# First FFN product of the last two token groups by Strassen's scheme, ELUs issued between the additions

## The chip, the cores and the metric

One core of a Trainium2 chip. The metric is the device time of one execution in microseconds (us); lower is better. PE is TensorE, DVE VectorE, ACT ScalarE, POOL GpSimd. PSUM is the memory, in banks, in which matmuls are summed; SBUF is the core's other memory. The granted clock is the share of its full clock that the profile shows TensorE to have had. A slack is the time by which something could come later before PE would wait.

## The reference

An attention with a threshold, then an FFN with ELU over its 4608 output rows of 512. The change concerns the FFN alone:

```python
n_tokens, d_model, d_ff = (4608, 512, 2048)
def _moe_ref(x, w_in, w_out):
    h = x @ w_in                                                     # first product
    g = np.where(h > 0.0, h, alpha * (np.exp(np.minimum(h, 0.0)) - 1.0))   # ELU, alpha = 1
    return (g @ w_out).astype(np.float32)                            # second product
```

## The kernel before

Tokens come in nine groups of 512: eight sequences, and a ninth group of the 64 last tokens of each. A group's FFN is interleaved with the next group's attention, except for the last two groups, which are left over at the end. A group is two chunks `c` of 256 tokens. `ffn1` is the plain first product, with the f tiles `u` and `u + 8` side by side; `ffn2` is the second product, by Strassen's scheme already.

```python
def ffn1(c, u):                                  # cut
    def part(k):                                 # k = 0, 1: f tile u, u + 8
        for j in range(KJ):                      # KJ = 4 tiles of d_model
            nc.tensor.matmul(loc["ph"][:, k], w_in_sb[:, j, ft * P : (ft + 1) * P],
                             xts[g][:, j, hf * CT : (hf + 1) * CT], start=(j == 0), stop=(j == KJ - 1))
    def exp():
        nc.scalar.activation(loc["g"], loc["h"], AF.Exp)                     # h is in PSUM
    def minus():
        nc.gpsimd.tensor_scalar(loc["g"], loc["g"], 1.0, -1.0, ALU.mult, ALU.add)
    def elu():
        nc.vector.scalar_tensor_tensor(loc["g"], loc["g"], 0.0, loc["h"], ALU.min, ALU.max)
        if u % 2 and c >= PLAIN:
            sums(c, u - 1)                       # four GpSimd sums for Strassen's second product

# the end of the program, after the last attention step
xts[B] = xpool.tile([P, KJ, MAIN], FP32, name="xt")
nc.sync.dma_start(xts[B], xtail.rearrange("j p n -> p j n"))
push_ffn(B)
while pending or units:
    finish_units(ffn_halves(1), slice(0, None))
    run_extra(99)
```

## Time and profile before

| | before |
|---|---|
| time, median of the first 3 runs | 1455.3 us (1453.4 to 1457.4) |
| profiled run | span 1449.4 us, granted clock 0.995 |
| last attention output copied (the last xt copy on ScalarE) | 1235.9 us |
| from there to the end of the span | 213.5 us |
| first and second product of a chunk in that stretch | 27.63 us and 24.17 us, PE alone |

### The profile page before, as it was taken

Reading aid. Unit: us, or ns where it says so; the run is one execution under the profiler, and the core shown is the slowest. Engines: PE = TensorE matmul, PEld = TensorE weight load, DVE = VectorE, ACT = ScalarE, POOL = GpSimd, SP = SyncE. Lnnn points to the kernel's source line nnn. Section 1 sums busy time; section 2 is a strip of 40 time slices with the busy share of each in tenths; the row PEclk is TensorE's granted clock in tenths of the full one; section 3 lists DMA queues with packets and bytes.
Section 4 is the critical chain, followed back from the end, with each engine's and each line's share of the span. In section 5 each row is a group of like instructions: output and inputs, shape, how many; then the busy total and the mean of one; then the engine's idle time right before and its main releaser. Section 6 shows DMA issues by size and latency. Waiting matters only on the chain.

```text
span 1449.4 us, 20329 instructions
## 1 busy us (share of the span) xinstructions
PE 1391.5 (96%) x6822; PEld 1037.2 (72%) x6822; DVE 878.9 (61%) x1910; ACT 439.7 (30%) x780; POOL 667.7 (46%) x1194
## 2 busy tenths in 40 slices
PE   7988778999999999999999999999999999999998
PEld 4555534647777777777777777777777778888887
DVE  6887665567676766677676767676767674111111
ACT  5665554323222322223222323232323231100100
POOL 4665554546444454535363626363535443313422
PEclk9999899999999999999999999999999999999999
DMA  4344442177677676667676767666767765100000
GB/s 95 78 93 117 111 123 84 51 193 188 184 185 195 174 202 183 190 181 185 183 197 171 189 190 191 182 189 180 195 182 192 192 172 148 45 15 8 8 15 15
DMA packets 298903, 205.44 MB, mean 142 GB/s; under 512 B 206384, under 2 KB 270384, under 8 KB 298800
## 3 DMA queue, kind: packets, MB, share of 16 engines
q1 hardware_dynamic: 298800, 204.15, 52.9%
q8 instruction: 54, 0.88, 0.2%
q14 instruction: 49, 0.40, 0.1%
HBM read 119.87 MB, written 84.21 MB: 141 GB/s over the span
## 4 chain that ended last, share of the span: by engine, by line
PE 82%; DVE 8%; POOL 4%; ACT 3%; issue 2%; DMA 1%; SPq 0%; POOLq 0%; DVEq 0%; ACTq 0%
PE ph L393 33%; PE po L494 24%; PE sc L220 12%; PE pv L347 8%; DVE w L247 2%; PE pv L343 2%; PE po L459 2%; ACT e L235 2%; POOL wtop L141 2%; DVE mx L230 2%; PE rt L259 1%; POOL w L256 1%; DVE wtop L136 1%; POOL nb L231 1%; DVE w_out_sb L145 1%
## 5 line engine op out<-in xcount | busy, mean ns | idle before, releaser
L393 PE MATMUL ph<-xt,w_in_sb 128*128 128x256 f32 x2304 | 521.5, 383 | 3.5 <-DVE w_in_sb L145 3.5
L393 PEld LDWEIGHTS ph<-xt,w_in_sb 128*128 128x128 f32 x2304 | 433.3, 190 | 83.9 <-issue 21.0
L235 ACT ACTIVATE e<-sc,nb,keep 128x576 f32<-128x576 f32 x288 | 227.6, 829 | 439.2 <-POOL nb L231 438.0
L230 DVE TENSOR_REDUCE mx<-sc 128x2 f32<-128x1152 f32 (+1 forms) x176 | 199.9, 1136 | 229.1 <-PE sc L220 229.0
L256 POOL TENSOR_SCALAR w<-w,rs 128x576 f32<-128x576 f32 x288 | 219.1, 771 | 223.5 <-DVE rs L250 217.3
L247 DVE SCALAR_TENSOR_TENSOR w<-sc,th,e 128x576 f32<-128x576 f32 x288 | 226.8, 815 | 78.3 <-ACT e L235 53.8
L220 PE MATMUL sc<-kT,qT 64*128 64x288 f32 x1024 | 180.3, 437 | 18.9 <-DVE w L247 9.1
L404 POOL TENSOR_SCALAR g<-g 128x512 f32<-128x512 f32 x144 | 89.7, 623 | 200.5 <-ACT g L401 199.3
L307 DVE STREAM_TRANSPOSE x<-w 128x512 f32<-128x512 f32 (+1 forms) x350 | 181.2, 567 | 0.9 <-POOL w L256 0.9
L231 POOL TENSOR_SCALAR nb<-mx,nkeep 128x2 f32<-128x2 f32 (+1 forms) x176 | 51.7, 294 | 265.1 <-DVE mx L230 257.6
L401 ACT ACTIVATE g<-ph 128x512 f32<-128x512 f32 x144 | 86.0, 597 | 266.2 <-PE ph L393 266.2
L408 DVE SCALAR_TENSOR_TENSOR g<-g,ph 128x512 f32<-128x512 f32 x144 | 97.0, 674 | 112.7 <-POOL g L404 112.6
L220 PEld LDWEIGHTS sc<-kT,qT 64*128 64x128 f32 x1024 | 99.3, 189 | 86.0 <-issue 53.1
L494 PE MATMUL po<-t,s 128*128 128x256 f32 x512 | 122.8, 386 | 4.5 <-DVE u L514 4.5
L494 PE MATMUL po<-w_out_sb,s 128*128 128x256 f32 x512 | 120.1, 384 | 0.0
L494 PE MATMUL po<-w_out_sb,g 128*128 128x256 f32 x512 | 117.7, 379 | 0.0
L494 PEld LDWEIGHTS po<-t,s 128*128 128x128 f32 x512 | 94.5, 190 | 28.9 <-DVE u L514 8.9
L494 PEld LDWEIGHTS po<-w_out_sb,s 128*128 128x128 f32 x512 | 95.4, 190 | 19.7 <-issue 4.7
L494 PEld LDWEIGHTS po<-w_out_sb,g 128*128 128x128 f32 x512 | 97.3, 190 | 13.9
L424 POOL TENSOR_TENSOR s<-g 128x256 f32<-128x256 f32 x128 | 93.2, 728 | 12.9 <-DVE g L408 12.9
L347 PE MATMUL pv<-wTb,vm 128*64 128x320 f32 x512 | 76.7, 439 | 0.0
L350 ACT COPY xt<-pv 128x256 f32<-128x256 f32 x64 | 23.8, 372 | 159.3 <-PE pv L347 159.2
(64 smaller groups left out, 1129.0 us busy)
## 6 DMA issues: line engine op xcount, KB each, us to landing
there<-x SPq DMA_DIRECT2D x500, 144.0 KB, 3.5
wTb<-there SPq DMA_DIRECT2D x75, 576.0 KB, 4.4
wTa<-there SPq DMA_DIRECT2D x50, 576.0 KB, 3.7
qm<-in_q_dram SPq DMA_DIRECT2D x128, 72.0 KB, 2.6
km<-in_k_dram SPq DMA_DIRECT2D x128, 72.0 KB, 3.6
vm<-in_v_dram SPq DMA_DIRECT2D x64, 128.0 KB, 2.5
wst<-in_moe_w_in_dram SPq DMA_DIRECT2D x16, 512.0 KB, 4.2
wst<-in_moe_w_out_dram SPq DMA_DIRECT2D x16, 512.0 KB, 3.8
```

Of the source, the lines that this page charges most:

```text
L220: nc.tensor.matmul(scs[h][:, a, :HALF], qs[r], kT[r, k0 : k0 + HALF], start=True, stop=True)
L230: nc.vector.tensor_reduce(st["mx"][:, cs], src[:, :, :, :HALF], axis=AX.XY, op=ALU.max)
L235: nc.scalar.activation(e, st[h][:, :, :HALF], AF.Exp, bias=st["nb"][:, h : h + 1], scale=keep)
L247: nc.vector.scalar_tensor_tensor(wv, sc[:, :, :HALF], st["th"][:, h : h + 1], e, ALU.is_ge, ALU.mult, accum_out=sm[:, h : h + 1])
L256: nc.gpsimd.tensor_scalar(wv, wv, st["rs"][:, h : h + 1], 1.0, ALU.mult, ALU.mult)
L307: nc.vector.transpose(x[:, :, c0 : c0 + nc_], src.rearrange("p (c g n) -> p g c n", c=nc_, n=T))
L347: nc.tensor.matmul(pv[h * D : (h + 1) * D, g0 * T : g1 * T], vm[:, h, c], wT[:, g0:g1, h * (NC + 1) + c], start=False, stop=(c == NC - 1), ...
L393: nc.tensor.matmul(loc["ph"][:, k], w_in_sb[:, j, ft * P : (ft + 1) * P], xts[g][:, j, hf * CT : (hf + 1) * CT], start=(j == 0), stop=(j = ...
L404: nc.gpsimd.tensor_scalar(loc["g"], loc["g"], 1.0, -1.0, ALU.mult, ALU.add)
L408: nc.vector.scalar_tensor_tensor(loc["g"], loc["g"], 0.0, loc["h"], ALU.min, ALU.max)
L424: nc.gpsimd.tensor_tensor(out, x, y, op)
L494: nc.tensor.matmul(cur[c, place], lhs, rhs, start=(begins and u == 0), stop=(u == NU - 1), skip_group_check=True)
```

## The change

Intent: for each pair of f tiles and all 512 tokens of a group, seven products of half size in place of eight. The sums of weights are made by VectorE late in the attention loop (six pairs) and inside the first group (two pairs), those of the inputs at the head of the first group and, for the second, under the first one's second product. Three accumulators X, Y, Z, each a whole PSUM bank, six banks in all. Each pair's exp and ELU are put off into the next pair. The core of the diff:

```diff
+        def first_product(g, u):
+            X, Y, Z = (psum["f"].tile([P, 512], FP32, name="po", tag="f")[:, :CT] for i in range(3))
+            h = hs[u % 2]                               # in SBUF
             ... # product(): two matmuls of 256 columns; kept(): copy or addition out of PSUM into SBUF
+            rest("exp0")                                # of the pair before, as all rest()
+            product(a11, b11, X, True)                  # 1
+            p1 = kept("s1", X)
+            rest("exp1")
+            product(a22, t4, Z, True)                   # 2
+            w1 = kept("w1", Z, p1)
+            rest("elu0")
+            product(a12, b21, X, False)                 # 3
+            nc.scalar.copy(h[:, 0, 0], X)
+            product(s2, t2, Y, True)                    # 4
+            u2 = kept("u2", Y, p1)
+            product(s1, t1, Z, True)                    # 5
+            t5 = kept("t5", Z, p1)
+            rest("elu1")
+            product(s3, t3, Y, False)                   # 6
+            nc.vector.tensor_tensor(h[:, 0, 1], Y, w1, ALU.add)
+            nc.vector.tensor_tensor(h[:, 1, 1], Y, t5, ALU.add)
+            product(s4, b22, Z, False)                  # 7
+            nc.vector.tensor_tensor(h[:, 1, 0], Z, u2, ALU.add)
             ...
-        push_ffn(B)
         while pending or units:
             finish_units(ffn_halves(1), slice(0, None))
             run_extra(99)
+        banks.close()
+        psum["f"] = ctx.enter_context(tc.tile_pool(name="ps_f3", bufs=6, space=PSUM))
+        input_sums(B - 1)                               # four 512-wide sums on VectorE
+        for g in (B - 1, B):
+            for u in range(NU):
+                if g < B and u in (2, 4):
+                    first_sums(u // 2 + 5)              # four weight sums of one pair
+                first_product(g, u)
+            flush()
             ... # then the second product; the odd chunk's sums are now on VectorE (3 of 4) and GpSimd
```

More of the change, by code (lines that the diff above doesn't have):

```diff
@@ L397, in exp @@
             if u == 0:
-                gs[c] = gpool.tile([P, NU, 2, 2, P], FP32, name="g")
-            loc["g"] = gs[c][:, u].rearrange("p j i t -> p (j i t)")
+                gs[c] = [gpool.tile([P, NU, 2, 2, P], FP32, name="g")]
+            loc["g"] = hidden(c, u, 1).rearrange("p u j i t -> p (u j i t)")
             loc["h"] = loc["ph"].rearrange("p k t -> p (k t)")
@@ L412, in ffn1, with hidden, sums @@
         return [lambda: part(0), lambda: part(1)], (exp, minus, elu)
-    def sums(c, u):
-        g = gs[c]
+    def hidden(c, u, n):
+        for g in gs[c]:
+            if u < g.shape[1]:
+                return g[:, u : u + n]
+            u -= g.shape[1]
+    def sums(c, u, engines=(nc.gpsimd,) * 4):
+        g = hidden(c, u, 2)
         def one(k):
@@ L419, in one @@
                 ss[c] = late["x"].tile([P, 4, NU, P], FP32, name="s", bufs=1)
-            (a11, a21), (a12, a22) = ([g[:, u : u + 2, j, i] for i in range(2)] for j in range(2))
+            (a11, a21), (a12, a22) = ([g[:, :, j, i] for i in range(2)] for j in range(2))
             s1, s2, s3, s4 = (ss[c][:, i, u : u + 2] for i in range(4))
@@ L423, in one @@
                              (s3, a11, a21, ALU.subtract), (s4, a12, s2, ALU.subtract))[k]
-            nc.gpsimd.tensor_tensor(out, x, y, op)
+            engines[k].tensor_tensor(out, x, y, op)
         extra.extend((0.8, c, lambda k=k: one(k)) for k in range(4))
@@ L458, in run @@
             for ft in range(4 * part + 2 * k, 4 * part + 2 * k + 2):
-                nc.tensor.matmul(cur[c, i][:, :DM], gs[c][:, ft % NU, ft // NU, i], w_out_sb[:, ft],
+                nc.tensor.matmul(cur[c, i][:, :DM], hidden(c, ft % NU, 1)[:, 0, ft // NU, i], w_out_sb[:, ft],
                                  start=(ft == 0), stop=(ft == NFT - 1))
@@ L488, in part @@
             for u in range(k * NU // 2, (k + 1) * NU // 2):
-                lhs = gs[c][:, u, left[1], left[2]] if left[0] == "g" else ss[c][:, left[1], u]
+                lhs = hidden(c, u, 1)[:, 0, left[1], left[2]] if left[0] == "g" else ss[c][:, left[1], u]
                 if right[0] == "w":
@@ L548, in behind @@
             values(pr, 0 if i == 1 else 1)
-        if i == NB - 1 and (pr + 1) % NPAIR == 0:
+        if i == NB - 1 and (pr + 1) % NPAIR == 0 and pr + 1 < NP:
             push_ffn(pr // NPAIR)
@@ L648 @@
     for name, bufs in (("s", 1), ("f", 3), ("t", 1)):
-        psum[name] = ctx.enter_context(tc.tile_pool(name=f"ps_{name}2", bufs=bufs, space=PSUM))
+        psum[name] = banks.enter_context(tc.tile_pool(name=f"ps_{name}2", bufs=bufs, space=PSUM))
     early.close()
@@ L654, with pieces_of, first_rooms, first_sums @@
         weight_sums(u, False)
+    def pieces_of(pool, name, shape, n, times=1, bufs=None):
+        for _ in range(times):
+            t = pool.tile(shape, FP32, name=name, bufs=bufs)
+            if len(shape) > 2:
+                axes = " ".join("abc"[: len(shape) - 1])
+                t = t.rearrange(f"p {axes} -> p ({axes})")
+            for x in range(0, t.shape[1] - n + 1, n):
+                yield t[:, x : x + n]
+    QN = 2 * P
+    rooms = []
+    def first_rooms():
+        rooms[:] = [*pieces_of(raw, "qm", [P, S // T, T], QN), *pieces_of(raw, "km", [P, S // T, T], QN),
+                    *pieces_of(qkp, "qT", [P, S], QN, 2), *pieces_of(qkp, "kT", [P, TAIL + S], QN, 2),
+                    *pieces_of(att, "e", [P, 2, HALF], QN, 2), *pieces_of(wpool[0], "w", [P, 2 * S], QN)]
+    sums_in = {}
+    def first_sums(u):
+        f0, f1 = (slice(f * P, (f + 1) * P) for f in (u, NU + u))
+        a11, a12, a21 = w_in_sb[:, :2, f0], w_in_sb[:, 2:, f0], w_in_sb[:, :2, f1]
+        s1, s2, s4 = sums_in[u] = [rooms.pop(0).rearrange("p (k f) -> p k f", k=2) for _ in range(3)]
+        nc.vector.tensor_tensor(s1, a21, w_in_sb[:, 2:, f1], ALU.add)
+        nc.vector.tensor_tensor(s2, s1, a11, ALU.subtract)
+        nc.vector.tensor_tensor(a21, a11, a21, ALU.subtract)
+        nc.vector.tensor_tensor(s4, a12, s2, ALU.subtract)
     QUOTA = ((2, 2), (2, 2), (2, 0), (2, 1), (2, 0))
@@ L672 @@
             run_extra(3.0)
+            if n > len(steps):
+                if n == len(steps) + 1:
+                    first_rooms()
+                for u in range(3 * (n - len(steps) - 1), 3 * (n - len(steps))):
+                    first_sums(u)
             if SWITCH < n <= len(steps):
@@ L693 @@
         finish_units(after, slice(0, None))
-        xts[B] = xpool.tile([P, KJ, MAIN], FP32, name="xt")
-        nc.sync.dma_start(xts[B], xtail.rearrange("j p n -> p j n"))
-        push_ffn(B)
         while pending or units:
@@ L699 @@
             run_extra(99)
+        banks.close()
+        psum["f"] = ctx.enter_context(tc.tile_pool(name="ps_f3", bufs=6, space=PSUM))
+        wide, narrow = wtp.tile([P, 3 * NT, NCH, T], FP32, name="wTb"), wtp.tile([P, 2 * NT, NCH, T], FP32, name="wTa")
+        wide, narrow = (t.rearrange("p g c n -> p (g c n)") for t in (wide, narrow))
+        g2 = [t.rearrange("p (u j i t) -> p u j i t", j=2, i=2, t=P) for t in (wide[:, : 12 * QN], narrow[:, : 4 * QN])]
+        rooms += [wide[:, 12 * QN : 13 * QN], narrow[:, 8 * QN : 9 * QN], *pieces_of(raw, "vm", [P, 2, NC, D], QN, bufs=2)]
@@ new lines, with input_sums @@
+        t2, t4 = (narrow[:, x * QN : (x + 2) * QN].rearrange("p (k t) -> p k t", k=2) for x in (4, 6))
+        (t3,) = pieces_of(raw, "vm", [P, 2, NC, D], 2 * QN, bufs=2)
+        t3 = t3.rearrange("p (k t) -> p k t", k=2)
+        hs = [h.rearrange("p (c j t) -> p c j t", c=2, j=2) for h in pieces_of(late["x"], "x", [P, NT, NCH, T], 4 * QN, 2, 2)]
+        def input_sums(g):
+            (b11, b12), (b21, b22) = ([xts[g][:, k : k + 2, t : t + CT] for t in (0, CT)] for k in (0, 2))
+            nc.vector.tensor_tensor(t3, b22, b12, ALU.subtract)
+            nc.vector.tensor_tensor(t2, t3, b11, ALU.add)
+            nc.vector.tensor_tensor(t4, b21, t2, ALU.subtract)
+            nc.vector.tensor_tensor(b12, b12, b11, ALU.subtract)
@@ new lines, in first_product, with product, kept, rest @@
+        def first_product(g, u):
+            f0, f1 = (slice(f * P, (f + 1) * P) for f in (u, NU + u))
+            (b11, t1), (b21, b22) = ([xts[g][:, k : k + 2, t : t + CT] for t in (0, CT)] for k in (0, 2))
+            s1, s2, s4 = sums_in[u]
+            a11, a12, s3, a22 = w_in_sb[:, :2, f0], w_in_sb[:, 2:, f0], w_in_sb[:, :2, f1], w_in_sb[:, 2:, f1]
+            X, Y, Z = (psum["f"].tile([P, 512], FP32, name="po", tag="f")[:, :CT] for i in range(3))
+            h = hs[u % 2]
+            def product(left, right, place, begins):
+                for k in range(2):
+                    nc.tensor.matmul(place, left[:, k], right[:, k], start=(begins and k == 0), stop=(k == 1),
+                                     skip_group_check=True)
+            def kept(name, x, y=None):
+                t = epool.tile([P, HM], FP32, name=name)
+                if y is None:
+                    nc.scalar.copy(t, x)
+                else:
+                    nc.vector.tensor_tensor(t, x, y, ALU.add)
+                return t
+            def rest(name):
+                if name in open_rest:
+                    open_rest.pop(name)()
+            rest("exp0")
[17 more added lines that the diff above has]
+            nc.vector.tensor_tensor(h[:, 1, 0], Z, u2, ALU.add)
+            def exp(c):
+                gt = hidden(2 * g + c, u, 1).rearrange("p u j i t -> p (u j i t)")
+                hc = h[:, c].rearrange("p j t -> p (j t)")
+                nc.scalar.activation(gt, hc, AF.Exp)
+                nc.gpsimd.tensor_scalar(gt, gt, 1.0, -1.0, ALU.mult, ALU.add)
+                open_rest[f"elu{c}"] = lambda: elu(c, gt, hc)
+            def elu(c, gt, hc):
+                nc.vector.scalar_tensor_tensor(gt, gt, 0.0, hc, ALU.min, ALU.max)
+                if c == 0 and u % 2:
+                    sums(2 * g, u - 1)
+                    run_extra(99)
+            open_rest["exp0"] = lambda: exp(0)
+            open_rest["exp1"] = lambda: exp(1)
@@ new lines, with flush @@
+        open_rest = {}
+        def flush():
+            for name in ("exp0", "exp1", "elu0", "elu1"):
+                open_rest.pop(name)()
+        input_sums(B - 1)
+        xts[B] = xpool.tile([P, KJ, MAIN], FP32, name="xt")
+        nc.sync.dma_start(xts[B], xtail.rearrange("j p n -> p j n"))
+        for g in (B - 1, B):
+            gs[2 * g] = [gpool.tile([P, NU, 2, 2, P], FP32, name="g")]
+            gs[2 * g + 1] = g2
+            for u in range(NU):
[3 more added lines that the diff above has]
+            flush()
+            for c in (2 * g, 2 * g + 1):
+                units.extend((ffn2, (c, m)) for m in range(7))
+                if c % 2:
+                    for u in range(0, NU, 2):
+                        sums(c, u, (nc.vector, nc.vector, nc.gpsimd, nc.vector))
+                    run_extra(99)
+                while pending or units:
+                    finish_units(ffn_halves(1), slice(0, None))
+                if c == 2 * B - 2:
+                    input_sums(B)
```

## The prediction

> **What bounds the kernel now.** I read the head of the page first, to see which engine is full and where.
>
> ```profile
> span 1449.4 us, 20329 instructions
> PE 1391.5 (96%) x6822; PEld 1037.2 (72%) x6822; DVE 878.9 (61%) x1910; ACT 439.7 (30%) x780; POOL 667.7 (46%) x1194
> ...
> PE   7988778999999999999999999999999999999998
> ...
> DVE  6887665567676766677676767676767674111111
> ```
>
> PE is busy almost throughout. The last six slices (36 us each) are what the change touches: PE stays at 9 while VectorE falls to 1. Attention is over and only the FFN of the last two token groups is left. The chain of waits in order of time is the second view (start, length, work):
>
> ```profile
> 1237.77 27.63 PE ph L393 x128
> 1265.40 24.17 PE po L494 x112
> 1289.57 27.63 PE ph L393 x128
> 1317.19 24.17 PE po L494 x112
> ...
> 1393.17 27.63 PE ph L393 x128
> 1420.80 24.19 PE po L494 x112
> 1444.98 0.02 issue
> 1445.01 0.42 DVE ot L504
> ```
>
> Each of the four chunks of 256 tokens is one piece for the first product and one for the second (already by Strassen's scheme), and nothing but PE is on the chain. 27.63 / 128 = 24.17 / 112 = 0.216 us a record, without a gap. So this end is PE at full rate: fewer matmuls shorten it, and any wait put into it lengthens it. Two traps lie here. The groups by line give 379 ns a matmul, the latency of a pipelined one, not its cost. And a record is not a matmul of the program:
>
> ```profile
> L393 PE MATMUL ph<-xt,w_in_sb 128*128 128x256 f32 x2304 | 521.5, 383 | 3.5 <-DVE w_in_sb L145 3.5
> ...
> L401 ACT ACTIVATE g<-ph 128x512 f32<-128x512 f32 x144 | 86.0, 597 | 266.2 <-PE ph L393 266.2
> ```
>
> The program calls eight first-product matmuls for each of the 144 exps, 1152 in all; the trace has 2304. Each fp32 matmul is two records, so one call of 256 columns costs 2 x 0.216 = 0.432 us. The timeline of the same stretch gives the other durations:
>
> ```profile
> 1266.11 0.62 POOL L404 TENSOR_SCALAR g<-g 128x512 f32<-128x512 f32 x1 [2.01 <-ACT g L401]
> 1266.76 0.69 DVE L408 SCALAR_TENSOR_TENSOR g<-g,ph 128x512 f32<-128x512 f32 x1 [1.94 <-POOL g L404]
> 1267.53 0.73 POOL L424 TENSOR_TENSOR s<-g 128x256 f32<-128x256 f32 x1 [0.81 <-DVE g L408]
> ...
> 1268.94 0.37 ACT L512 COPY s<-po 128x256 f32<-128x256 f32 x1 [2.91 <-PE po L494]
> ...
> 1286.15 0.42 DVE L504 TENSOR_TENSOR ot<-po,t 128x256 f32<-128x256 f32 x1 [3.03 <-PE po L494]
> 1286.49 0.41 DVE L504 TENSOR_TENSOR ot<-po,w 128x256 f32<-128x256 f32 x1
> ```
>
> Exp 0.60 (the row above), its "minus one" on GpSimd 0.62, the ELU 0.69, a GpSimd sum 0.73, a ScalarE copy 0.37, an addition out of PSUM 0.42. Two queued additions start 0.34 apart; elsewhere in the trace queued ELUs take 0.60 of the queue and GpSimd sums 0.69. Handovers from engine to engine are 0.03 to 0.09. A product's reader starts some 0.44 us after the start of its last record (the copy above at 1268.94, that record at 1268.47), so 0.22 after PE is free for the next.
>
> **What the Trainium skill says.** (1) "TensorE: Matmul & The Clock Gate", Back-to-back issue gap: 256 columns take 262 cycles warm, an estimate of 109 ns; "Perfetto Trace Analysis", Engine Utilization, halves PE's rate for an fp32 mode. The trace agrees with the halved rate for one record (216 ns); neither passage speaks of the two records a call. (2) The same TensorE page, Architectural detail: ScalarE and VectorE are strict FIFO. An ELU that isn't ready then holds up every addition behind it. No line of this trace tests it; the change depends on it. (3) "SBUF — State Buffer", Who interferes with whom: a VectorE instruction with two SBUF inputs and a GpSimd one that reads SBUF exclude each other; with one SBUF input (the other in PSUM) they don't. The trace agrees: an operation of median 0.69 us took 1.23 where it met GpSimd's:
>
> ```profile
> 46.47 0.75 POOL L256 TENSOR_SCALAR w<-w,rs 128x576 f32<-128x576 f32 x1
> 46.53 1.23 DVE L145 SCALAR_TENSOR_TENSOR w_in_sb<-wst,wtop 128x512 f32<-128x512 f32 x1 [1.64 <-ACT wTa L274]
> ```
>
> **The change part by part.** *Removed from PE.* For one pair of f tiles and 512 tokens the plain product is 16 calls, Strassen's seven products are 14. Two groups of eight pairs: 2 x 8 x 2 = 32 calls x 0.432 = 13.8 us. A pair takes 14 x 0.432 = 6.05 us instead of 6.91, a group 48.4 instead of 55.3. That is the whole possible gain, 0.95%. The second product keeps its matmuls.
>
> *Added work, by rate.* VectorE gets six additions a pair beside its two ELUs: 6 x 0.34 + 2 x 0.60 = 3.2 us in 6.05. ScalarE: two exps and two copies, 1.9. GpSimd: two "minus ones" and half of the even chunk's four sums in two pairs, 1.2 + 1.4 = 2.6. None comes near PE.
>
> *Added waits.* A product that accumulates into a used bank waits for the reader of the partial sum. One product lasts 2 x 0.432 = 0.86. Product 3 (bank X) waits for the copy of product 1: 0.22 + 0.37 + 0.06 = 0.65 after product 1's end, with product 2 between: slack 0.21. Product 5 (Z) waits for w1, read after product 2, with two products between: 1.73 - (0.22 + 0.42 + 0.06) = 1.03. Product 6 (Y) waits for u2, read after product 4, and product 7 (Z) for t5, read after product 5: each 0.86 - 0.70 = 0.16. All hide, three of them barely. Each must also find its engine free. The even ELU stands between w1 and u2, whose data come 1.73 apart, and the two take 0.34 + 0.69: slack 0.7. The odd ELU stands after t5: 0.34 + 0.60 = 0.94 in the 0.86 until the next product's data; it delays the first addition into h by about 0.1, and then exp, ahead of the next pair's copy in ScalarE's queue, still has 0.6 to spare. So nothing stalls in the ideal order, but the ELU now reads h from SBUF, excludes GpSimd, and can lose 0.6 to 0.7 to it, which is just these slacks. I take 0.1 us a pair, 16 x 0.1 = +1.6, in a range of 0 to 5.
>
> *Weight sums.* 24 VectorE additions of 256 columns, about 24 x 0.4 = 10 us, run in the last steps of the attention loop where VectorE is idle: after 1217 us the trace has only the second product's additions on it, 3 us or more apart. Free. The last eight come inside the first group, four before pair 2 and four before pair 4, 1.6 us each on VectorE before a w1 with 1.03 of slack: +0.3 each, +0.6.
>
> *Start.* Product 1 needs plain inputs, product 2 needs t4, three dependent 512-wide sums at 0.72 = 2.2 us, which VectorE begins only after the group before has had its last addition; that one ends at 1238.2 in the old trace, PE begins the new group at 1237.6. So t4 comes at 1240.4, PE is done with product 1 at 1238.5: +1.9 once. The second group's input sums lie under the second product.
>
> *Between the products.* The last pair's even ELU must be there for the eighth call of the second product, 7 x 0.432 = 3.0 us in. h's first addition comes 0.2 before product 7 ends, then exp, "minus one" and ELU, 0.60 + 0.62 + 0.69 and handovers = 2.4 us: in time. The odd chunk's 16 sums (12 on VectorE, 5 us, in the first group behind 2.9 us of input sums) are needed from 10.4 us into that chunk: hidden.
>
> Sum: -13.8 + 1.6 + 0.6 + 1.9 = -9.7 us: 1455.3 - 9.7 = 1445.6, say 1446 us.
>
> **The rivals.** *A: all hides.* Only the start is paid: 1443. For: no engine above 55% in a pair. Against: slacks of 0.16 us, less than one handover counted twice. *B: the waits become the loop.* If results come 0.2 us later than I count (one more handover, or weights loaded only after the wait: the trace has 1.99 instead of 1.89 us for eight records after a stall), products 3, 6 and 7 each stall by 0.1 to 0.2: 16 x 0.45 = 7 us, 1451. *C: ELU against GpSimd.* If ELUs meet GpSimd's sums in half the pairs and each costs PE 0.6: 8 to 16 x 0.6 = 5 to 10 us, 1449 to 1454. *D: a new bound elsewhere*, say the buffers reused for weight sums coming free late, or the start waiting for the old PSUM banks: several us once, 1452. B and C together would eat the gain: 1458.
>
> **Range and chances.** The floor is 1455.3 - 13.8 = 1441.5; repeated runs of one kernel spread by 4 us. I say 1446, with 1441 to 1455 for 8 in 10. Faster by over 2% (below 1426) is more than all matmuls saved: 0.01. Slower by over 2% would need 43 us of new waits, 2.7 a pair: 0.02. Within 2%: 0.97.
>
> **What would show it.** Right: the first product of a group is some 48 to 50 us in the chain of waits, nearly all PE, with VectorE or ScalarE pieces only at the start; 448 records less 0 to 2%; the idle time before its matmuls is under 3 us, of which 1.9 at the start on the input sums; the second product stays at 24.2 a chunk. Wrong: a group of 52 us or more with idle time put down to u2, t5 and the copy (B); ELUs with a mean well over 0.69 and stalls in the pairs that follow an odd one (C); or a long stall at the group's beginning on something other than t4 (D).

## The result and the profile after

Five runs: 1440.8 us median (1437.8 to 1443.0), before in the same rounds 1455.3 (1453.4 to 1457.4). The ratio is 0.9898, 95% interval 0.9879 to 0.9917. The gain of 14.5 us is more than the 13.8 us that I had called the whole possible gain, and the time lies just below my range of 1441 to 1455.

The head of the page after:

```profile
span 1436.0 us, 20455 instructions
PE 1377.6 (96%) x6758; PEld 1023.8 (71%) x6758; DVE 949.1 (66%) x2070; ACT 451.2 (31%) x812; POOL 660.6 (46%) x1170
...
DVE  6887665567677667766776767676777677563542
```

VectorE is no longer idle in the last six slices; PE has 64 records fewer, which is 32 calls. The chain of waits after, from the end of the attention on (start, length, work):

```profile
1234.28 1.94 PE po L500 x8
...
1236.58 0.69 DVE vm L751
...
1237.30 0.70 DVE wTa L752
...
1238.03 0.70 DVE wTa L753
...
1238.77 47.75 PE po L766 x220
1286.52 48.35 PE po L500 x224
1334.87 48.35 PE po L766 x224
1383.21 48.36 PE po L500 x224
```

L766 is the first product, L500 the second. A group's first product is 48.35 us, 224 x 0.216, against 55.3 before; the second is unchanged. At the start the chain leaves PE for three input sums, as predicted. What PE itself waited for in the whole stretch (waited for; total us, times, longest):

```profile
PE po L766 <- DVE wTa L753: 0.9, 1, 0.9
PE po L766 <- DVE ot L510: 0.6, 1, 0.6
```

Both are at the start. This view leaves out short waits (it lists none of the 16 stalls of 0.27 us in experiment 4 below); that PE waited for nothing after the start rests on the chain, where 224 records fill 48.35 us. How close that was shows in one pair, on PE and VectorE:

```profile
1246.64 1.03 PE L766 MATMUL po<-wTa,qT 128*128 128x256 f32 x4
...
1247.51 1.03 PE L766 MATMUL po<-xt,km 128*128 128x256 f32 x4
1247.71 0.42 DVE L774 TENSOR_TENSOR u<-po,s 128x256 f32<-128x256 f32 x1 [0.45 <-PE po L766]
...
1248.37 1.03 PE L766 MATMUL po<-vm,w_in_sb 128*128 128x256 f32 x4
```

The rows are product 4 into Y, product 5 into Z, the addition u2 that reads Y, product 6 into Y. u2 ends at 1248.13 and needs 0.06 us to be seen; product 6 starts at 1248.37, without a stall. The slack is 0.18 us, where I had reckoned 0.16.

Where does 14.5 us come from, then? The two profiled spans are 13.4 us apart. The span can be cut at the last xt copy, which ends the common part. Before that cut the two traces show the same instructions in the same order on every engine, but for the 24 weight sums on VectorE from 1216 us on, which move nothing: the difference of the two profiles is 1.6 us at the copy before them and at the one after.

| profiled run | last xt copy starts | from there to the end |
|---|---|---|
| before | 1235.9 | 213.5 |
| after | 1234.3 | 201.7 |

The stretch that the change touches gives 11.8 us; 1.6 us of this pair of profiles lie ahead of it, in code that did not change. That asked for a test of the scatter.

### The profile page after: what moved, and what is told of

It reads as the page before. It is cut to its first block, busy times and chain, and to the rows that moved or that the text cites. A ratio compares the mean times of both kernels' runs of the same rounds, so it can differ in the third digit from the quotient of the medians.

```text
span 1436.0 us, 20455 instructions
## 1 busy us (share of the span) xinstructions
PE 1377.6 (96%) x6758; PEld 1023.8 (71%) x6758; DVE 949.1 (66%) x2070; ACT 451.2 (31%) x812; POOL 660.6 (46%) x1170
## 4 chain that ended last, share of the span: by engine, by line
PE 82%; DVE 8%; POOL 4%; ACT 3%; issue 2%; DMA 1%; SPq 0%; POOLq 0%; DVEq 0%
PE ph L393 26%; PE po L500 24%; PE sc L220 12%; PE pv L347 8%; PE po L766 7%; DVE w L247 2%; PE pv L343 2%; PE po L465 2%; ACT e L235 2%; DVE mx L230 2%; POOL wtop L141 2%; PE rt L259 1%; POOL w L256 1%; DVE wtop L136 1%; POOL nb L231 1%
## 5 line engine op out<-in xcount | busy, mean ns | idle before, releaser
L393 PE MATMUL ph<-xt,w_in_sb 128*128 128x256 f32 x1792 | 409.3, 383 | 3.2 <-DVE w_in_sb L145 3.2
L393 PEld LDWEIGHTS ph<-xt,w_in_sb 128*128 128x128 f32 x1792 | 335.3, 190 | 70.2 <-issue 21.0
L500 PE MATMUL po<-t,s 128*128 128x256 f32 x512 | 122.8, 386 | 4.5 <-DVE u L520 4.5
L500 PE MATMUL po<-w_out_sb,s 128*128 128x256 f32 x512 | 120.1, 384 | 0.0
L500 PEld LDWEIGHTS po<-t,s 128*128 128x128 f32 x512 | 94.6, 190 | 28.9 <-DVE u L520 8.9
L500 PEld LDWEIGHTS po<-w_out_sb,s 128*128 128x128 f32 x512 | 95.4, 190 | 19.7 <-issue 4.7
L401 ACT ACTIVATE g<-ph 128x512 f32<-128x512 f32 x112 | 66.9, 597 | 130.5 <-PE ph L393 130.5
L500 PE MATMUL po<-w_out_sb,g 128*128 128x256 f32 x448 | 103.2, 379 | 0.0
L404 POOL TENSOR_SCALAR g<-g 128x512 f32<-128x512 f32 x112 | 70.3, 627 | 67.4 <-ACT g L401 66.3
L500 PEld LDWEIGHTS po<-w_out_sb,g 128*128 128x128 f32 x448 | 85.1, 190 | 12.2
L408 DVE SCALAR_TENSOR_TENSOR g<-g,ph 128x512 f32<-128x512 f32 x112 | 75.0, 670 | 18.0 <-POOL g L404 17.9
L430 POOL TENSOR_TENSOR s<-g 128x256 f32<-128x256 f32 x112 | 82.6, 738 | 3.9 <-DVE g L810 3.9
```

Source lines behind the costliest of these rows:

```text
L430: engines[k].tensor_tensor(out, x, y, op)
L500: nc.tensor.matmul(cur[c, place], lhs, rhs, start=(begins and u == 0), stop=(u == NU - 1), skip_group_check=True)
```

## The experiments

In all tables "end" is the time from the last xt copy to the end of the span.

**1, 2 and 10: both kernels again, unchanged.** Theory: what exceeds 11.9 us is scatter of the first part. Rival: the changed program really runs its first part faster, by where its instructions or buffers lie. No edit.

> The kernel before, unchanged, run as if it were a variant. Theory chance (the surplus of some 2.6 us over the 11.9 us that the last stretch explains is scatter of the first 230 us, where the weights are loaded): ratio 1.000, the interval within 0.998 and 1.002, and the last xt copy ahead of the last stretch (1235.9 us in the profile before, 1234.3 in the profile after) moves by 1 us or more from profile to profile of the same kernel. Rival placement (the changed program really runs its first part faster): this copy stays at 1235.9 within 0.3 us.

> The changed kernel, unchanged, again. Theory chance: the true gain is the last stretch's, 32 calls x 0.432 = 13.8 less 1.9 at the start = 11.9 us, ratio 0.9918, so a new measurement comes back from 0.9898 towards 0.992. Rival placement: 0.9900 again, with the last xt copy at 1234.3 again. In both, the last stretch of the profile repeats: 49.7, 48.4, 48.4, 48.4 us.

> The changed kernel a third time, to compare with the next kernel in the same rounds and to have one more draw of the scatter: ratio 0.9918, between 0.990 and 0.9935; last stretch 49.7, 48.4, 48.4, 48.4 us; whatever else it differs by arises in the first 250 us.

| run | ratio to before (95%) | last xt copy | end |
|---|---|---|---|
| 1, before again | 0.9983 (0.9969 to 0.9996) | 1238.6 | 213.5 |
| 2, after again | 0.9918 (0.9904 to 0.9932) | 1241.2 | 201.7 |
| 10, after a third time | 0.9916 (0.9900 to 0.9931) | 1237.9 | 201.7 |

The end repeats to 0.1 us in every profile of the same kernel; the last xt copy does not. It was at 1235.9 and 1238.6 us in two profiles of the kernel before, and at 1234.3, 1241.2 and 1237.9 in three of the kernel after. The rival falls. The kernel before differed from itself by 0.17%, and its interval leaves out 1; my expectation for it (within 0.998 and 1.002) held for the ratio, but its interval reached lower. So an interval from so few runs can be too narrow, also the first comparison's, which just leaves out the 0.9919 that 11.8 us would be. The last xt copy in the timelines of after, then of after again:

```profile
1234.33 0.37 ACT L350 COPY xt<-pv 128x256 f32<-128x256 f32 x1 [14.67 <-PE pv L347]
```

```profile
1241.22 0.37 ACT L350 COPY xt<-pv 128x256 f32<-128x256 f32 x1 [14.67 <-PE pv L347]
```

Half of the difference arises in the first 35 us. The windows of 20 to 30 us (stretch, its length, then for each engine busy us and instructions; then the granted clock, the DMA share, GB/s), after and after again:

```profile
20.00:30.00 10.00, 9.46 (x48) 5.96 (x49) 9.50 (x31) 7.45 (x13) 6.86 (x18) 1.00 0.35 57
```

```profile
20.00:30.00 10.00, 10.00 (x31) 6.71 (x30) 7.22 (x21) 5.27 (x10) 4.67 (x13) 0.54 0.20 33
```

The granted clock was 1.00 in one and 0.54 in the other, and PE was busy throughout in the slow one with two thirds of the matmuls. In before again that column reads 1.00 for the same stretch, but five matmuls of one shape are as slow there. The timelines of after, after again and before again:

```profile
22.77 0.77 PE L259 MATMUL rt<-ident,w 128*128 128x128 f32 x5
```

```profile
20.43 1.33 PE L259 MATMUL rt<-ident,w 128*128 128x128 f32 x5
```

```profile
21.03 1.33 PE L259 MATMUL rt<-ident,w 128*128 128x128 f32 x5
```

So the slow start belongs to neither kernel, and the clock column did not show it in every profile. The rest arises between 140 and 250 us, where the granted clock dips in every profile but not alike (from 160 to 180 us it is 0.97 in after and 0.69 in after again). The Trainium skill, "TensorE: Matmul & The Clock Gate", What's actually happening, has a half-rate clock until PE has been busy for a free-running window, so a start that varies from run to run is what it leads one to expect; that the clock is the whole cause of the scatter is not shown.

**3 and 11: input sums earlier.** The start cost is the wait for the input sums, which stand in VectorE's queue behind the last addition. They can go ahead of the second product's last half. Product 1 must then not wait for that addition through the exchange of banks, so the old three banks are kept.

```diff
             ... # the pool of the three banks stays open; cut
-        banks.close()
-        psum["f"] = ctx.enter_context(tc.tile_pool(name="ps_f3", bufs=6, space=PSUM))
-        while pending or units: ...          # the last half of the second product
         input_sums(B - 1)
+        while pending or units: ...
```

> The changed kernel with the input sums of the first Strassen group issued before the second product's last half instead of after it, and with the three PSUM banks of the second product kept for X, Y and Z instead of six new ones. Theory (the start cost of 1.9 us is the wait for the input sums behind VectorE's last addition; the bank count does not matter because each bank has 0.16 us of slack even with three): 1.9 us faster than the changed kernel, first group 48.4 us instead of 49.7 and starting at once. Rival (three banks are too few, each pair's products 2 and 4 wait for the additions of the pair before): the start is gained, but 16 pairs lose 0.1 to 0.3 us each, so 0 to 3 us slower than that.

> The changed kernel with the input sums issued before the second product's last half and three banks, again: its profile repeats 48.5, 48.4, 48.4, 48.4 us without a start wait, 1.9 us faster than the changed kernel in the chain; the ratio 0.9905, between 0.989 and 0.992, so that the difference to the changed kernel is visible in the profile rather than in the intervals.

Ratios 0.9901 (0.9888 to 0.9915) and 0.9903 (0.9890 to 0.9917); end 199.9 us both times, 1.8 us less than the changed kernel. The chain of waits of experiment 3:

```profile
1235.75 1.92 PE po L500 x8
1237.67 48.48 PE po L761 x224
```

PE passes from the second product of the old group to the first of the new one without a gap (0.13 us of the first group's 48.48 are lost at its second product). So the start cost was the input sums, and three banks do for X, Y and Z. The ratio's interval overlaps that of the changed kernel; the profiles tell them apart. Medians: 1440.6 and 1440.0 us against 1443.1 and 1441.7 for the changed kernel in the same rounds. This is the best version.

**6: three banks alone.** Experiment 3 changed two things; this takes only the banks.

```diff
             ... # the pool of the three banks stays open; cut
-        banks.close()
-        psum["f"] = ctx.enter_context(tc.tile_pool(name="ps_f3", bufs=6, space=PSUM))
```

> The changed kernel with the second product's three PSUM banks kept for X, Y and Z instead of six new ones, nothing else. Theory: no pair waits for a bank (the last addition of a pair leaves Z 0.16 us before the next pair's product 2 wants it), and the start is bound by the input sums, so product 2 of the first pair starts when it did: the same time within 1.5 us, groups of 49 to 50 and 48.4 us, the 0.6 us wait for the old banks gone from product 1 but added to product 2's wait. Rival (the banks' change was the start cost): 0.6 to 1.9 us faster. Rival (three banks are too few): 2 to 5 us slower.

Ratio 0.9915 (0.9902 to 0.9929), end 201.7 us: the same as after. PE's wait at the start became one of 1.7 us on the input sums:

```profile
PE po L764 <- DVE wTa L751: 1.7, 1, 1.7
```

The count of banks is neither the cost nor the gain.

**4: u2 and t5 twice.** More work is put where the slacks are thin, to see whether they are as thin as reckoned.

```diff
                     nc.vector.tensor_tensor(t, x, y, ALU.add)
+                    if name in ("u2", "t5"):
+                        nc.vector.tensor_tensor(t, x, y, ALU.add)
```

> The changed kernel with the additions u2 and t5 done twice (same result). Theory of the prediction (slack of products 6 and 7 is 0.16 us each): the second addition ends 0.34 us later, so each of the two products stalls by 0.18 us plus 0.1 for the late weights: 16 x 2 x 0.28 = 9 us slower than the changed kernel, with PE idle before products 6 and 7. Rival (results come earlier than I counted, slack of 0.4 us or more): under 2 us slower.

Ratio 0.9958 (0.9946 to 0.9971), end 207.8: 6.1 us slower than after, not 9. The timeline of one pair, u2 and its copy, product 6, product 7:

```profile
1266.02 0.42 DVE L774 TENSOR_TENSOR u<-po,s 128x256 f32<-128x256 f32 x1 [0.45 <-PE po L766]
1266.48 0.42 DVE L776 TENSOR_TENSOR u<-po,s 128x256 f32<-128x256 f32 x1
...
1266.96 1.13 PE L766 MATMUL po<-vm,w_in_sb 128*128 128x256 f32 x4
...
1267.92 1.03 PE L766 MATMUL po<-xt,kT 128*128 128x256 f32 x4
```

Product 6 would have started at 1266.69 (product 5's start at 1265.82 and four records) and starts at 1266.96, 0.06 after the second addition: a stall of 0.27 us. It then takes 0.96 us until product 7 in place of 0.86, because its weights came after the wait. 0.37 x 16 = 5.9 us. Product 7 does not stall: the delay of product 6 has already given t5 the time. My 9 us counted two stalls where the first covers the second, and took each as 0.28 us: the copy of u2 started 0.46 us after the first in place of 0.34. The slack itself was right.

**5: each ELU at once.** Exp, minus one and ELU at the end of their own pair, ahead of everything of the next.

```diff
-            rest("exp0")   # and rest("exp1"), rest("elu0"), rest("elu1")
             ...
             open_rest["exp1"] = lambda: exp(1)
+            flush()
```

> The changed kernel with each exp, minus one and ELU issued at the end of its own pair, ahead of all of the next pair, instead of between the next pair's additions. Theory (VectorE and ScalarE take their work strictly in order, and slacks are those of the prediction): the odd ELU ends about 4.0 us after product 6 of its pair, so the next pair's w1 starts 1.1 us late, more than its 1.03 of slack, and product 5 stalls by 0.1 to 0.2 plus 0.1 for the weights in 14 pairs: 2 to 4 us slower than the changed kernel, PE idle before product 5, put down to w1. Rival (order does not matter, the engines have room): within 1 us of the changed kernel.

Ratio 1.0013 (0.9990 to 1.0036), end 216.1: 14.4 us slower than after, more than the change had gained. The second group's first product takes 51.0 us, 2.7 more than 48.35, where the 2 to 4 us that I expected of both groups together meant 1 to 2; the first takes 59.5 in place of 47.75 after the start wait. There the weight sums meet the late ELUs. Its timeline, an odd ELU, the last of four weight sums, w1, product 5:

```profile
1271.35 1.21 DVE L806 SCALAR_TENSOR_TENSOR wTb<-wTb,x 128x512 f32<-128x512 f32 x1 [0.51 <-POOL wTb L802]
...
1275.08 0.41 DVE L689 TENSOR_TENSOR vm<-w_in_sb,vm 128x256 f32<-128x256 f32 x1
1275.41 0.41 DVE L774 TENSOR_TENSOR w<-po,s 128x256 f32<-128x256 f32 x1
...
1275.88 2.00 PE L766 MATMUL po<-xt,e 128*128 128x256 f32 x4 [3.33 <-DVE w L774]
```

The ELU, 0.69 us when alone, takes 1.21 beside a GpSimd sum; four weight sums follow (0.83 to 0.94 us for three of them in place of 0.42); w1 comes last, and PE has waited 3.33 us. Then its four records take 2.00 us in place of 1.03: the granted clock was 0.50 from 1276 to 1278 us. That happened twice (waits of 3.32 and 3.33 us).

**9: each ELU at once, weight sums moved out.** To see whether that meeting is the cause.

```diff
-                if g < B and u in (2, 4):
-                    first_sums(u // 2 + 5)
             ...
+        first_sums(6)
+        first_sums(7)
         input_sums(B - 1)
```

> The kernel with each ELU issued at the end of its own pair, and in addition the last eight weight sums of the first group moved from pairs 2 and 4 to before the input sums. Theory (in that kernel the second group, without weight sums, lost 2.7 us and the first 11.7, because four weight sums on top of the late ELU and its exclusion by GpSimd held w1 up by 3.3 us twice, after which PE ran at half clock): the first group's 14 products a pair now lose 2.7 us as the second's do, the granted clock stays at 1.0, and the start waits 2.9 us more for the eight sums: 8 us slower than the changed kernel instead of 14. Rival (the first group is slow for another reason): its pairs lose 9 us or more again.

Ratio 0.9985 (0.9970 to 1.0000), end 212.9: 11.2 us slower than after, not 8. After the start the view of waits lists six on w1 of at most 0.41 us, three in each group, so the long ones are gone and the meeting was their cause. From 1260 us on the first group's remaining 168 records take 38.7 us, 2.5 more than 168 x 0.216. What I had missed is the start: PE now waits 3.79 us for the input sums, and its next 52 records take 14.6 us in place of 11.2, at a granted clock of 0.50 from 1245 to 1251 us. The start and one of the six, in the timeline:

```profile
1245.40 2.07 PE L766 MATMUL po<-wTa,w_in_sb 128*128 128x256 f32 x4 [3.79 <-DVE wTa L753]
...
1263.86 1.13 PE L766 MATMUL po<-xt,qT 128*128 128x256 f32 x4 [0.41 <-DVE w L774]
```

So the order of the ELUs alone costs 2.5 and 2.7 us in the two groups, some 5 us; the rest of experiment 5's 14.4 is its meeting with the weight sums and the half clock that follows. My "the granted clock stays at 1.0" was wrong.

**8: GpSimd's sums twice.** More work for GpSimd, to test the rival that ELUs and GpSimd collide.

```diff
             engines[k].tensor_tensor(out, x, y, op)
+            if c >= 2 * B - 2 and c % 2 == 0:
+                engines[k].tensor_tensor(out, x, y, op)
```

> The changed kernel with the four GpSimd sums of the even chunk done twice in the last two groups (same result). Theory (GpSimd has room as it is, but a queue of eight sums, 5.6 us and more where ELUs exclude them, makes the next minus one 3 us late, and the ELU behind it holds up u2): in three pairs of each group product 6 stalls by some 0.9 us, 5 us slower than the changed kernel, range 3 to 9, PE idle before product 6 in pairs 2, 4 and 6. Rival (GpSimd is far from mattering): within 1 us.

Ratio 0.9992 (0.9977 to 1.0008), end 212.7: 11.0 us slower than after. The timeline, the even chunk's minus one, its ELU, u2, product 6:

```profile
1263.43 0.62 POOL L808 TENSOR_SCALAR g<-g 128x512 f32<-128x512 f32 x1
...
1264.08 1.08 DVE L812 SCALAR_TENSOR_TENSOR g<-g,x 128x512 f32<-128x512 f32 x1 [2.17 <-POOL g L808]
1265.09 0.41 DVE L776 TENSOR_TENSOR u<-po,s 128x256 f32<-128x256 f32 x1
...
1265.56 1.13 PE L768 MATMUL po<-vm,w_in_sb 128*128 128x256 f32 x4 [1.57 <-DVE u L776]
```

The exp was done at 1260.15; the minus one waited 3.3 us behind sums, the ELU waited for it and then took 1.08 us beside the next minus one, u2 waited for the ELU and PE for u2. That is the strict order of VectorE's queue, on which the prediction counted and which it could not test: u2, ready for some 1.9 us, stayed behind an ELU that was not (product 4's last record starts at 1262.75 us, and readers came 0.44 after such a start elsewhere). The mechanism and the place, six pairs, are as expected. From record to record PE lost 1.65 to 1.73 us each time (the bracket counts from the modelled end of the last record), and 0.1 for the weights, 10.6 us of the 11.0; I had expected 0.9 a pair. That the ELU itself was stretched, which I had left out, is 0.4 us of the difference, and that the minus one waited 3.3 us in place of 3 is another 0.3.

**7: the last group alone.** The group before it keeps the plain product, from the same three banks; the weight sums go under the second product of its odd chunk.

```diff
             ... # the three banks stay, and so does group B - 1 in push_ffn; its weight sums in the loop go; cut
-        input_sums(B - 1)
+        while pending or units:                 # group B - 1, plain
+            finish_units(ffn_halves(1), slice(0, None))
+            run_extra(99)
+            if len(units) < 7 and done <= NU:
+                first_sums(done) if done < NU else input_sums(B)
+                done += 1
-        for g in (B - 1, B):
+        for g in (B,):
```

> Strassen's scheme for the first product of the last group alone; the group before keeps the plain product. All 32 weight sums lie under that group's second product, and so do the input sums. Theory (the gain is matmul records and nothing else): 16 calls x 0.432 = 6.9 us faster than the kernel before, ratio 0.9953, first products of 55.3 and 48.4 us in the chain, no start stall. Rival (there is a gain beside the matmuls, in the attention part or from a lighter schedule): clearly more than half of what the full change gives, 0.994 or less.

Ratio 0.9953 (0.9941 to 0.9965), end 206.7: 6.8 us less than before, for 6.9 expected. The end of its chain of waits, a plain and a Strassen first product among them:

```profile
1290.57 27.63 PE ph L393 x128
...
1342.37 48.38 PE po L759 x224
1390.74 48.36 PE po L500 x224
```

The gain is proportional to the calls saved, with nothing beside it.

## Why the prediction was right or wrong

*The gain on PE: right.* 32 calls at 0.432 us; the profile has 64 records fewer, and the two first products are 48.35 us where they were 55.3. Seeing that a call is two records was decisive: with 0.216 us a call, a pair would have been 3.0 us of PE against 3.2 of VectorE, and the change would have looked like a loss.

*The slacks: right, but the guess laid on top of them wrong.* I found that nothing stalls in the ideal order, with 0.16 us to spare at products 6 and 7, and then took "+1.6 us" for ELUs that lose time to GpSimd. They do lose it: the even chunk's have a median of 0.88 us where the same stretch of before had 0.69, and the odd chunk's reach 1.26. PE never felt it. This term measured 0. The step that failed is "I take 0.1 us a pair". I had reckoned 0.7 us of slack for the even ELU and 0.6 behind the odd one; the even ones lost 0.2 and the odd ones at most 0.6, so no pair paid anything. In the pair shown above VectorE still waited 0.45 us for product 4 after a slowed even ELU.

*The weight sums inside the first group: +0.6 predicted, 0 measured.* I had set 1.6 us of sums against 1.03 us of slack, as if they began when w1's data came. In pair 2 they began at 1250.64 us, right behind the pair before, and w1's data came at some 1252.05 (product 2's last record and 0.44); w1 started at 1252.40. So 0.35 of the 1.03 us went, although one sum was stretched to 0.71 us while GpSimd was at work.

*The start: +1.9 predicted,* and experiment 3 recovered 1.8.

*Between the products: right,* no wait appears there.

So the stretch itself gained 11.8 us where my sum said 9.7: the two small additions, 2.2 us together, are the terms that were mis-sized; each measured 0. I had put a price on risks whose slack I had just shown to be there.

*The range failed for a second reason.* The step is "The floor is 1455.3 - 13.8 = 1441.5; repeated runs of one kernel spread by 4 us", followed by a low end of 1441. It treated the median of three runs before as exact and allowed half a microsecond below the floor. The first comparison gave 14.5 us, 2.7 more than the profile of the stretch supports, by the luck of the draw; repeated twice, the ratio came to 0.9918 and 0.9916, and 0.9917 x 1455.3 = 1443.2 us, within the range. Experiments 1, 2 and 10 show that the part ahead of the change moved by up to 6.9 us between profiles. A floor of work saved is no floor for a measured difference.

*The rivals.* A, all hides but the start, predicted 1443 and is what happened. B and C (the waits become the loop; ELU against GpSimd) did not occur, but experiments 4, 5 and 8 show that they are near: two more VectorE additions a pair cost 6 us, the simpler ELU order 14 with the weight sums where they are, doubled sums on GpSimd 11. D, new banks or late buffers: experiment 6 shows no effect of the banks' exchange on the end.

What stays open: what sets PE's rate in the first 250 us from run to run, and whether it is all of the scatter.

## What to carry to other kernels

When PE is full, price a removed matmul by the spacing of its records in the chain of waits times the records per call, and compare each added wait with the products that lie between the bank's last write and its next use. Keep late work of an in-order engine out of the way of what frees a bank: the order in which the ELUs were issued was worth some 5 us of the 11.8 here, and with the weight sums behind them all of it, while no engine but PE was near full. To measure a change of under 1%, cut the span where the common part ends and compare the rest.

## What the Trainium skill lacked or had wrong

- "TensorE: Matmul & The Clock Gate", Back-to-back issue gap, and "Perfetto Trace Analysis", Engine Utilization: neither says that one fp32 matmul call leaves two records. Here 1152 calls left 2304, each 0.216 us, so 0.432 us a call of 256 columns. ("FP8 and Floating Point Precision" does say that true fp32 makes four passes; how they show in a trace is on no page that I found.)
- No page that I read says that a matmul which waits for a PSUM bank also has its weights late. After each stall four records took 1.13 in place of 1.03 us, so a stall costs 0.1 us more than the wait.
- "TensorE: Matmul & The Clock Gate", HAM oscillation, puts the idle time that halves the clock above about 3.4 us. Nothing here contradicts it: waits of 3.32, 3.33 (experiment 5) and 3.79 us (experiment 9) were followed by a granted clock of 0.50, and waits of 1.57 us (experiment 8) were not. These waits count from the modelled end of the last record, 0.16 us after the next one was due, so PE stood still that much longer.
- The same page counts the start's ramp as under 1% of a typical kernel and calls it variable from run to run. The part of this kernel ahead of the change moved by up to 6.9 us in 1440, 0.5%, but that is more than half of what the change gains; that this limits a comparison is not said.
